# QKV of the first block in two passes of 256 tokens, its tiles normalised one by one, and the last tile's output in unequal columns on two queues: a fused attention and GLU layer on one core

## The chip, the cores and the metric

The kernel runs on one core of one Trainium2 chip. The metric is the device time of one launch in microseconds (us), the median of several launches. One run of each kernel is also profiled: the profile has every instruction of every engine with its start and its duration. A run is called slow when it is over 1.5% above the fastest run of the same kernel, else fast; the record also gives the mean clock that PE was granted in each run, as a share of full speed. PE is the tensor engine (matmuls), VectorE is DVE in the profile, ScalarE is ACT, GpSimd is POOL, and SP issues DMAs. A ratio of two kernels is the mean time of one kernel's fast runs over the mean of the other's fast runs of the same rounds on the same chip, so it is not quite the ratio of the medians that I quote.

## The reference

```python
xn = layernorm(x)                                   # x: 2048 tokens x 512
q, k, v = split_heads(xn @ wqkv)                    # 32 heads of 16
logits = q . k[pos - 2 * w] / 4, w = 0..7           # a window of 8 keys, dilation 2
s = (softmax(logits) . v[pos - 2 * w]) @ wo
h = gelu(xn @ w_gate) * (xn @ w_up)                 # 512 -> 1792
y = h @ w_down
out = x + s * silu(y)
```

All tensors are bf16. Tokens are worked on in four blocks of 512 (j = 0..3), each of four tiles of 128.

## The kernel before

Each piece of work is a task with an engine, an estimated duration and dependences. A list scheduler in the Python program runs the tasks in an imagined time and so fixes the **order** of instructions on every engine; on the chip the engines follow that order and wait for each other by semaphores. A change in one part can therefore move instructions in every later part.

The names in the profiles: tr is a transpose of a normalised tile xn_t on PE, xnT its copy. prod is a product of q and k on VectorE, and an L reduction is the 16 matmuls that add such products up to logits. sum, rs and b are the softmax's sums, their reciprocals and the spreading of these over partitions. pv is a product of attention weights and v on VectorE, and an O reduction is the 16 matmuls that add those up. In the feed-forward part (FFN), g and u are the two products with w_gate and w_up, and hT is gelu(g) * u on VectorE.

The first block's QKV, before: both halves of q, then of k, then of v; a PSUM bank holds one chunk of 128 output channels for 512 tokens, filled in two halves. The code here is shortened (`...`).

```python
def qkv(j):
    for which in range(3):                       # q, k, v
        mms = []
        if j == 0:
            for half in range(2):
                for c in range(NC):              # NC = 4 chunks
                    mms.append(add_main(2 * MM, ... qkv_mm(0, which, c, half * 256, (half + 1) * 256),
                        deps=[copied[2 * half], copied[2 * half + 1]] + [(w_there[which], 0.0)], ...))
            mms = mms[NC:]
        ...                                      # other blocks: 512 tokens at once
        for c in range(NC):
            e = add("act", ACT1, ... qkv_evacuate(j, which, c), deps=[mms[c]], ...)
```

Layer norm, before: block 0's reciprocal roots in pairs through ScalarE's square root, all other blocks' by four on GpSimd.

```python
if j == 0:
    for half in range(2):
        pair = list(ts)[2 * half : 2 * half + 2]
        r = rstd_act(pair[0], 2, [stat(t) for t in pair])
        for t in pair:
            transpose(t, norm(t, r), on_act=t % 2 == 0)
else:
    r = rstd_done[j] = rstd_pool(ts[0], TPB, [stat(t) for t in ts])
    ...
```

V goes to DRAM (vT_dram) and comes back per block and half as v_arr, four loads of 260 KB each, into three buffers, so the fourth v_arr can only be issued when the first has been used up. w_down (1.8 MB) is loaded by ScalarE's queue:

```python
start(wd_sb[:], B_w_down.rearrange("(k p) n -> p k n", p=P), q_ready[3])
```

The last tile's tail: s in two halves of 256 columns, each with its gate (silu(y) * s), its residual and its store, both stores on SP.

The softmax here doesn't subtract the row's maximum and nothing guards it: scores larger than these inputs give would overflow.

## Time and profile before

| | before |
|---|---|
| timed runs, median | 240.33 us |
| profile used for the prediction | span 242.5 us, launch 244.24 us, a slow one |
| PE busy | 94% of the span |
| VectorE busy | 65% |
| first QKV matmul / block 1's first QKV matmul | 8.39 us / 23.26 us |
| PE's waits between 70 and 97 us | about 2.8 us |

The busy shares are from the page's first line, and the last two rows are read from PE's rows of the timeline and from the list of waits. The profile was 1.6% slower than the timed runs.

### The profile page before, as it was taken

What the parts mean: (1) busy time and instruction counts of PE and PEld (TensorE: products, weight loads), DVE (VectorE), ACT (ScalarE), POOL (GpSimd) and SP (SyncE); (2) the same over time, 40 slices, a digit from 0 to 9 for tenths busy, and PEclk for the clock granted to TensorE, in tenths of its full rate; (3) what the DMA queues carried; (4) which work ended last, traced back from release to release, by engine and by line L of the source; (5) the groups of instructions that cost most, each with busy time, mean ns of one, the idle gap of its engine ahead of it and who ended that gap; (6) DMA issues with size and microseconds to landing.
All of it is one profiled execution on the core that took longest, in us unless ns stands there. A gap on an engine that the chain in (4) does not pass through costs nothing.

```text
span 242.5 us, 3469 instructions
## 1 busy us (share of the span) xinstructions
PE 228.9 (94%) x1337; PEld 106.0 (44%) x1360; DVE 157.1 (65%) x234; ACT 108.6 (45%) x162; POOL 30.2 (12%) x70
## 2 busy tenths in 40 slices
PE   7886999999988998999999999999999999999992
PEld 2675544444333433444444444444444444444441
DVE  4597999999969999996749953144342234343131
ACT  2353576477843685403683241182324142325100
POOL 7122930303332100120000000000000000000000
PEclk9999999999999999999999999999999999999999
DMA  4993799399997700091000000100000100000001
GB/s 146 347 374 133 161 205 371 86 199 311 226 288 177 167 3 0 0 195 48 23 0 3 0 0 22 43 24 0 0 1 3 43 22 22 3 0 0 22 29 39
DMA packets 14545, 22.66 MB, mean 93 GB/s; under 512 B 1328, under 2 KB 11456, under 8 KB 14528
## 3 DMA queue, kind: packets, MB, share of 16 engines
q0 software_dynamic: 2592, 8.54, 15.9%
q1 hardware_dynamic: 8208, 7.60, 10.0%
q10 hardware_dynamic: 3728, 6.29, 8.3%
q8 instruction: 10, 0.16, 0.3%
q14 instruction: 7, 0.06, 0.1%
HBM read 18.22 MB, written 4.21 MB: 92 GB/s over the span
## 4 chain that ended last, share of the span: by engine, by line
PE 78%; DVE 9%; DMA 6%; issue 2%; SPq 2%; DVEq 0%
PE y_ps L732 20%; PE u_ps L678 17%; PE g_ps L678 17%; PE qkv_ps L398 13%; DMA x_sb<-in_A_x_dram 6%; PE s_ps L720 6%; DVE prod L507 4%; PE O_ps L631 3%; PE L_ps L520 2%; DVE hT L695 2%; SPq L203 1%; DVE pv L617 1%; PE tr_ps L355 1%; SPq L198 1%; PE b_ps L584 1%
## 5 line engine op out<-in xcount | busy, mean ns | idle before, releaser
L695 DVE TENSOR_TENSOR hT<-gl,u_ps 128x512 bf16<-128x512 bf16 x56 | 38.2, 684 | 33.6 <-PE u_ps L678 28.0
L678 PE MATMUL g_ps<-xnT,wg_sb 128*128 128x512 bf16 x221 | 57.0, 379 | 1.3 <-DVE hT L695 0.8
L678 PE MATMUL u_ps<-xnT,wu_sb 128*128 128x512 bf16 x216 | 56.5, 379 | 0.4 <-issue 0.2
L688 ACT ACTIVATE gl<-g_ps 128x512 bf16<-128x512 f32 x56 | 33.4, 597 | 50.0 <-PE g_ps L678 45.3
L732 PE MATMUL y_ps<-wd_sb,hT 128*128 128x512 bf16 x218 | 50.2, 379 | 0.3
L398 PE MATMUL qkv_ps<-xnT,wqkv_sb 128*128 128x512 bf16 (+1 forms) x234 | 44.4, 336 | 3.2 <-DVE xnT L363 1.8
L617 DVE TENSOR_TENSOR pv<-attn,v_arr 128x2048 bf16<-128x2048 bf16 x32 | 37.9, 1220 | 2.8 <-DMA v_arr<-vT_dram 2.6
L507 DVE TENSOR_TENSOR prod<-q_sb,k_sb 128x2048 bf16<-128x2048 bf16 x32 | 37.8, 1217 | 0.0
L746 DVE TENSOR_TENSOR sg<-sil,s_ps 128x512 bf16<-128x512 bf16 (+1 forms) x17 | 11.0, 655 | 36.2 <-PE s_ps L720 25.0
L678 PEld LDWEIGHTS <-wg_sb 128*128 128x128 bf16 x224 | 21.5, 98 | 27.6 <-issue 2.6
L732 PEld LDWEIGHTS <-hT 128*128 128x128 bf16 x224 | 21.8, 98 | 26.7 <-issue 0.4
L678 PEld LDWEIGHTS <-wu_sb 128*128 128x128 bf16 x224 | 21.4, 98 | 26.8 <-issue 1.9
L398 PEld LDWEIGHTS <-wqkv_sb 128*128 128x128 bf16 x240 | 22.2, 98 | 20.2 <-issue 2.1
L743 ACT ACTIVATE sil<-y_ps 128x512 bf16<-128x512 f32 x16 | 9.6, 597 | 47.7 <-PE y_ps L732 47.7
L486 POOL DMA_DIRECT2D v_arr<-vT_dram x32 | 18.7, 589 | 62.2 <-DVE pv L617 37.5
L720 PE MATMUL s_ps<-wo_sb,o_sb 128*128 128x512 bf16 (+1 forms) x68 | 16.4, 367 | 0.0
L307 DVE BATCH_NORM_STATS2 stats<-x_sb 128x6 f32<-128x512 bf16 x16 | 10.8, 675 | 5.0 <-DMA x_sb<-in_A_x_dram 5.0
L411 ACT ACTIVATE q_sb<-qkv_ps 128x512 bf16<-128x512 f32 x16 | 9.2, 598 | 6.9 <-PE qkv_ps L398 6.9
L413 ACT ACTIVATE k_sb<-qkv_ps 128x512 bf16<-128x512 f32 x16 | 9.2, 599 | 4.9 <-PE qkv_ps L398 4.8
L418 ACT ACTIVATE vst<-qkv_ps 128x512 bf16<-128x512 f32 x16 | 9.1, 603 | 4.8 <-PE qkv_ps L398 4.7
L720 PEld LDWEIGHTS <-o_sb 128*128 128x128 bf16 x68 | 6.7, 98 | 7.4
L642 ACT ACTIVATE o_sb<-O_ps 128x1024 bf16<-128x1024 f32 x8 | 8.2, 1022 | 3.3 <-PE O_ps L631 2.8
(55 smaller groups left out, 116.1 us busy)
## 6 DMA issues: line engine op xcount, KB each, us to landing
v_arr<-vT_dram POOLq DMA_DIRECT2D x32, 260.0 KB, 6.9
vT_dram<-vst SPq DMA_DIRECT2D x16, 128.0 KB, 7.4
out_dram<-sg SPq DMA_DIRECT2D x15, 128.0 KB, 1.7
wg_sb<-in_B_w_gate_dram ACTq DMA_DIRECT2D x1, 1792.0 KB, 12.1
wu_sb<-in_B_w_up_dram ACTq DMA_DIRECT2D x1, 1792.0 KB, 12.7
wd_sb<-in_B_w_down_dram ACTq DMA_DIRECT2D x1, 1792.0 KB, 18.7
wqkv_sb<-in_A_wqkv_dram SPq DMA_DIRECT2D x3, 512.0 KB, 7.6
x_sb<-in_A_x_dram SPq DMA_DIRECT2D x3, 512.0 KB, 10.2
```

The source lines that it names most:

```text
L307: nc.vector.bn_stats(out=stats[:, t, :], in_=x_sb[:, t, :])
L398: nc.tensor.matmul(tiles["qkv", j, fo][:, lo:hi], lhsT=wqkv_sb[:, dk, fo * P : (fo + 1) * P], rhs=xnT[:, dk, j * TQ + lo : j * TQ + hi], s ...
L486: nc.gpsimd.dma_start(out=v_arr[32 * w4 : 32 * (w4 + 1), :, :], in_=src)
L507: nc.vector.tensor_tensor(out=prod[:], in0=tiles["q", j][:, c, :].unsqueeze(1).to_broadcast([P, 4, TQ]), in1=kwin, op=ALU.mult,)
L617: nc.vector.tensor_tensor(out=pv[:], in0=tiles["attn", j][:, w2, :].unsqueeze(1).to_broadcast([P, 4, TQ]), in1=tiles["va", j, half][:, 4 * ...
L678: nc.tensor.matmul(ps[:], lhsT=w[:, dk, fc * P : (fc + 1) * P], rhs=xnT[:, dk, j * TQ : (j + 1) * TQ], start=(dk == 0), stop=(dk == NC - 1),)
L688: nc.scalar.activation(out=tiles["gl", j, fc][:], in_=tiles["g_ps", j, fc][:], func=AF.Gelu_apprx_tanh)
L695: nc.vector.tensor_tensor(out=tiles["h", j][:, fc, :], in0=tiles["gl", j, fc][:], in1=tiles["u_ps", j, fc][:], op=ALU.mult,)
L720: nc.tensor.matmul(tiles["s", t][:, cs], lhsT=tiles["o", j][:, c, tt * P : (tt + 1) * P], rhs=wo_sb[:, c, cs], start=(c == 0), stop=(c == ...
L732: nc.tensor.matmul(tiles["y", t][:], lhsT=tiles["h", j][:, fc, tt * P : (tt + 1) * P], rhs=wd_sb[:, fc, :], start=(fc == 0), stop=(fc == N ...
L743: nc.scalar.activation(out=tiles["sil", t][:], in_=tiles["y", t][:], func=AF.Silu)
L746: nc.vector.tensor_tensor(out=tiles["sg", t][:, cs], in0=tiles["sil", t][:, cs], in1=tiles["s", t][:, cs], op=ALU.mult,)
```

## The change

The intent: keep PE fed at the start. Tiles of block 0 are normalised singly, so that the first reaches PE sooner; QKV runs all of q, k, v for the first 256 tokens, then for the second 256, with two chunks in each bank; x's second block comes in two halves, the rest of x later; three warm-up matmuls less; and, not in the change's name, block 1's roots go through ScalarE in pairs instead of GpSimd. At the end, 384 and 128 columns, the second store on ScalarE's queue, each residual right behind its gate.

```diff
-    lnpool = pool("lnpool", 3)
+    lnpool = pool("lnpool", 4)
...
     load_wqkv(0)
     load_wqkv(1)
-    load_x(1)
+    load_x(4, 6)
     load_wqkv(2)
-    load_x(2)
-    load_x(3)
+    load_x(6, 8)
+    load_x(8, 12)
+    load_x(12, 16)
...
-    for _ in range(12):
+    for _ in range(9):
         nc.tensor.matmul(warm_ps[:], lhsT=warm[:, 0:P], rhs=warm[:], start=True, stop=True)
...
         if j == 0:
+            behind = []
+            for half in range(2):
+                pair = list(ts)[2 * half : 2 * half + 2]
+                for t, s in [(t, stat(t, behind)) for t in pair]:
+                    transpose(t, norm(t, rstd_act(t, 1, [s])), on_act=t % 2 == 0)
+                behind = [copied[t] for t in pair if t % 2 == 1]
+        elif j == 1:
             for half in range(2):
                 pair = list(ts)[2 * half : 2 * half + 2]
                 r = rstd_act(pair[0], 2, [stat(t) for t in pair])
                 for t in pair:
-                    transpose(t, norm(t, r), on_act=t % 2 == 0)
+                    transpose(t, norm(t, r), on_act=False)
...
     def qkv(j):
+        w = 2 if j == 0 else 1
+        n = TQ // w
+        for lo in range(0, TQ, n):
+            for which in range(3):
+                for c in range(0, NC, w):
...                              (matmuls of w chunks into one bank, one eviction of [w, n])
...
-            nc.sync.dma_start(out=out2d[t * P : (t + 1) * P, cs], in_=tiles["sg", t][:, cs])
+            q = nc.scalar if split and cs.stop == D else nc.sync
+            q.dma_start(out=out2d[t * P : (t + 1) * P, cs], in_=tiles["sg", t][:, cs])
-        n = D // parts
-        columns = [slice(p * n, (p + 1) * n) for p in range(parts)]
+        edges = (0, D) if not split else (0, D - P, D)
+        columns = [slice(a, b) for a, b in zip(edges, edges[1:])]
```

More of the change, by code (lines that the diff above doesn't have):

```diff
@@ L177 @@
     order = Order(
-        {"xn": 3, "q": 3, "vst": 4, "va": 3, "pr": 6, "attn": 2, "o": 2, "h": 1, "gl": 3, "sg": 3,
+        {"xn": 4, "q": 3, "vst": 4, "va": 3, "pr": 6, "attn": 2, "o": 2, "h": 1, "gl": 3, "sg": 3,
          "f": 4, "a": 2, "O": 1}
@@ L200, in load_wqkv, with load_x @@
         )
-    def load_x(j):
+    def load_x(t0, t1):
         nc.sync.dma_start(
-            out=x_sb[:, j * TPB : (j + 1) * TPB, :],
-            in_=x2d[j * TQ : (j + 1) * TQ, :].rearrange("(t p) d -> p t d", p=P),
+            out=x_sb[:, t0:t1, :], in_=x2d[t0 * P : t1 * P, :].rearrange("(t p) d -> p t d", p=P)
         )
@@ L209 @@
     load_wqkv(1)
-    load_x(1)
+    load_x(4, 6)
     load_wqkv(2)
-    load_x(2)
-    load_x(3)
-    x_there = [3.2, 3.5, 3.8, 4.1] + [10.0] * 4 + [13.0] * 4 + [16.0] * 4
-    w_there = [7.0, 8.5, 11.5]
+    load_x(6, 8)
+    load_x(8, 12)
+    load_x(12, 16)
+    x_there = [3.2, 3.5, 3.8, 4.1] + [9.5] * 2 + [12.0] * 2 + [13.5] * 4 + [16.0] * 4
+    w_there = [7.0, 8.5, 11.0]
     warm = cpool.tile([P, TQ], BF16, name="warm")
@@ L291 @@
     warm_ps = psa.tile([P, TQ], F32, name="warm_ps", tag="a")
-    for _ in range(12):
+    for _ in range(9):
         nc.tensor.matmul(warm_ps[:], lhsT=warm[:, 0:P], rhs=warm[:], start=True, stop=True)
-    order.clock["pe"] = 5.6
+    order.clock["pe"] = 5.0
     copied = {}
@@ L303, in layer_norm, with stat @@
         rs = {}
-        def stat(t):
+        def stat(t, behind=()):
             def fn():
@@ L308, in fn @@
                 nc.vector.bn_aggr(out=mv[:, t, :], in_=stats[:, t, :])
-            return add("dve", STATS, fn, deps=[(x_there[t], 0.0)], prio=prio)
+            return add("dve", STATS, fn, deps=[(x_there[t], 0.0), *behind], prio=prio)
         def rstd_act(t0, n, deps):
@@ L320, in rec @@
                 nc.vector.reciprocal(out=rstd[:, t0 : t0 + n, 0], in_=rstd[:, t0 : t0 + n, 0])
-            a = add("act", 0.25, sq, deps=deps, prio=prio, func="sqrt")
-            return add("dve", 0.08, rec, deps=[a], prio=prio - 0.01)
+            a = add("act", 0.3, sq, deps=deps, prio=prio, func="sqrt")
+            return add("dve", 0.15, rec, deps=[a], prio=prio - 0.01)
         def rstd_pool(t0, n, deps):
@@ L346, in fn @@
                 )
-            return add("dve", NORM, fn, deps=[dep], prio=prio, takes=[("xn", t)])
+            return add("dve", NORM, fn, deps=[dep], prio=prio - 0.01, takes=[("xn", t)])
         def transpose(t, dep, on_act):
@@ L391 @@
     v_stored = {}
-    def qkv_mm(j, which, c, lo, hi):
-        fo = which * NC + c
-        if lo == 0:
-            tiles["qkv", j, fo] = psf.tile([P, TQ], F32, name="qkv_ps", tag="f")
-        for dk in range(NC):
-            nc.tensor.matmul(
-                tiles["qkv", j, fo][:, lo:hi],
-                lhsT=wqkv_sb[:, dk, fo * P : (fo + 1) * P],
-                rhs=xnT[:, dk, j * TQ + lo : j * TQ + hi],
-                start=(dk == 0),
-                stop=(dk == NC - 1),
-            )
@@ L406, in qkv_evacuate @@
-    def qkv_evacuate(j, which, c):
-        ps = tiles["qkv", j, which * NC + c]
-        if which == 0:
-            if c == 0:
-                tiles["q", j] = qpool.tile([P, NC, TQ], BF16, name="q_sb", tag="q")
-            nc.scalar.activation(out=tiles["q", j][:, c, :], in_=ps[:], func=AF.Copy, scale=SCALE)
-        elif which == 1:
-            nc.scalar.activation(
-                out=k_sb[:, c, PAD + j * TQ : PAD + (j + 1) * TQ], in_=ps[:], func=AF.Copy
-            )
-        else:
-            tiles["vst", j, c] = vpool.tile([P, TQ], BF16, name="vst")
-            nc.scalar.activation(out=tiles["vst", j, c][:], in_=ps[:], func=AF.Copy)
@@ L420, in qkv @@
-    def qkv(j):
-        for which in range(3):
-            mms = []
-            if j == 0:
-                for half in range(2):
-                    for c in range(NC):
-                        ts = (2 * half, 2 * half + 1)
-                        mms.append(
-                            add_main(
-                                2 * MM,
-                                lambda c=c, half=half, which=which: qkv_mm(
-                                    0, which, c, half * TQ // 2, (half + 1) * TQ // 2
-                                ),
-                                deps=[copied[t] for t in ts] + [(w_there[which], 0.0)],
-                                takes=[("f", ("qkv", 0, which, c))] if half == 0 else [],
-                            )
-                        )
-                mms = mms[NC:]
-            else:
-                for c in range(NC):
-                    mms.append(
-                        add_main(
-                            4 * MM,
-                            lambda c=c, which=which: qkv_mm(j, which, c, 0, TQ),
-                            deps=[copied[t] for t in range(j * TPB, (j + 1) * TPB)],
-                            takes=[("f", ("qkv", j, which, c))],
-                        )
-                    )
-            for c in range(NC):
-                takes = []
-                if which == 0 and c == 0:
-                    takes = [("q", j)]
-                if which == 2:
-                    takes = [("vst", (j, c))]
-                e = add(
-                    "act", ACT1, lambda c=c, which=which: qkv_evacuate(j, which, c), deps=[mms[c]],
-                    prio=-0.5, takes=takes, frees=[("f", ("qkv", j, which, c))],
-                )
-                if which == 0:
-                    q_ready[j] = e
-                elif which == 1:
-                    k_ready[j] = e
-                else:
-                    def store(c=c):
-                        nc.sync.dma_start(
-                            out=vT_dram[c * P : (c + 1) * P, PAD + j * TQ : PAD + (j + 1) * TQ],
-                            in_=tiles["vst", j, c][:],
-                        )
-                    st = add("sp", 0.6, store, deps=[e], prio=-1.0, frees=[])
-                    v_stored[j] = add(("dma", j, c), 3.0, lambda: None, deps=[(st, 0.0)], frees=[("vst", (j, c))])
@@ new lines, in store_v, with fn, mms, evacuate @@
+    def store_v(j, c, lo, n, w):
+        def fn():
+            o = vT_dram[c * P : (c + w) * P, PAD + j * TQ + lo : PAD + j * TQ + lo + n]
+            nc.sync.dma_start(
+                out=o.rearrange("(w p) n -> p w n", p=P),
+                in_=tiles["vst", j, c, lo][:].rearrange("p (w n) -> p w n", w=w),
+            )
+        return fn
+    def qkv(j):
+        w = 2 if j == 0 else 1
[3 more added lines that the diff above has]
+                for c in range(0, NC, w):
+                    key = (j, which, c, lo)
+                    def mms(key=key, which=which, c=c, lo=lo):
+                        ps = psf.tile([P, TQ], F32, name="qkv_ps", tag="f")
+                        tiles["qkv", key] = ps
+                        for i in range(w):
+                            fo = which * NC + c + i
+                            for dk in range(NC):
+                                nc.tensor.matmul(
+                                    ps[:, i * n : (i + 1) * n],
+                                    lhsT=wqkv_sb[:, dk, fo * P : (fo + 1) * P],
+                                    rhs=xnT[:, dk, j * TQ + lo : j * TQ + lo + n],
+                                    start=(dk == 0),
+                                    stop=(dk == NC - 1),
+                                )
+                    def evacuate(key=key, which=which, c=c, lo=lo):
+                        ps = tiles["qkv", key][:].rearrange("p (w n) -> p w n", w=w)
+                        if which == 0:
+                            if c == 0 and lo == 0:
+                                tiles["q", j] = qpool.tile([P, NC, TQ], BF16, name="q_sb", tag="q")
+                            nc.scalar.activation(
+                                out=tiles["q", j][:, c : c + w, lo : lo + n], in_=ps, func=AF.Copy,
+                                scale=SCALE,
+                            )
+                        elif which == 1:
+                            at = PAD + j * TQ + lo
+                            nc.scalar.activation(
+                                out=k_sb[:, c : c + w, at : at + n], in_=ps, func=AF.Copy
+                            )
+                        else:
+                            tiles["vst", j, c, lo] = vpool.tile([P, TQ], BF16, name="vst")
+                            nc.scalar.activation(
+                                out=tiles["vst", j, c, lo][:], in_=tiles["qkv", key][:], func=AF.Copy
+                            )
+                    there = [(w_there[which], 0.0)] if j == 0 else []
+                    m = add_main(
+                        4 * MM, mms,
+                        deps=[copied[t] for t in range((j * TQ + lo) // P, (j * TQ + lo + n) // P)] + there,
+                        takes=[("f", ("qkv", *key))],
+                    )
+                    takes = [("vst", key)] if which == 2 else []
+                    if which == 0 and c == 0 and lo == 0:
+                        takes = [("q", j)]
+                    e = add(
+                        "act", ACT1, evacuate, deps=[m], prio=-0.5, takes=takes,
+                        frees=[("f", ("qkv", *key))],
+                    )
+                    if which == 0:
+                        q_ready[j] = e
+                    elif which == 1:
+                        k_ready[j] = e
+                    else:
+                        st = add("sp", 0.6, store_v(j, c, lo, n, w), deps=[e], prio=-1.0)
+                        v_stored[j] = add(
+                            ("dma", key), 3.0, lambda: None, deps=[(st, 0.0)], frees=[("vst", key)]
+                        )
@@ L709, in ffn_pair, with out_tile @@
         )
-    def out_tile(j, tt, parts):
+    def out_tile(j, tt, split):
         t = j * TPB + tt
@@ L777, in add_s @@
                 add_main(
-                    4 * MM / parts, lambda cs=cs: s_mms(cs), deps=[o_ready[j]],
+                    4 * MM * (cs.stop - cs.start) / D, lambda cs=cs: s_mms(cs), deps=[o_ready[j]],
                     takes=[("f", ("s", t))] if cs.start == 0 else [],
@@ L797, in out_tile @@
             d = add(
-                "dve", 0.68 / parts, lambda cs=cs: gate(cs), deps=[a, sm], prio=-1.8,
+                "dve", 0.06 + 0.62 * (cs.stop - cs.start) / D, lambda cs=cs: gate(cs), deps=[a, sm], prio=-1.8,
                 frees=[("f", ("s", t))] if end else [],
             )
-            d = add("dve", 0.37 / parts, lambda cs=cs: residual(cs), deps=[d], prio=-1.6)
-            st = add("sp", 0.6, lambda cs=cs: store(cs), deps=[d], prio=-0.5)
+            d = add(
+                "dve", 0.06 + 0.31 * (cs.stop - cs.start) / D, lambda cs=cs: residual(cs), deps=[d],
+                prio=-1.9 if split else -1.6,
+            )
+            st = add("act" if split and end else "sp", 0.6, lambda cs=cs: store(cs), deps=[d], prio=-0.5)
             add(("dma", "out", t, cs.start), 2.0, lambda: None, deps=[(st, 0.0)], frees=[("sg", t)] if end else [])
@@ L838 @@
         for tt in range(TPB):
-            out_tile(j, tt, 2 if j == NJ - 1 and tt == TPB - 1 else 1)
+            out_tile(j, tt, j == NJ - 1 and tt == TPB - 1)
     order.run()
```

## The prediction

> **What bounds the kernel now.** I read first the page's shares, then PE's waits, then the chain of work that ended last, then the timeline of the first 30 us, and last the stretch from 66 to 97 us, where VectorE and TensorE trade places.
>
> ```profile
> PE 228.9 (94%) x1337; PEld 106.0 (44%) x1360; DVE 157.1 (65%) x234; ACT 108.6 (45%) x162; POOL 30.2 (12%) x70
> ...
> PE qkv_ps L398 <- DVE xnT L363: 1.8, 1, 1.8
> PE warm_ps L293 <- DVE eps_sb L221: 1.2, 1, 1.2
> PE qkv_ps L398 <- DMA wqkv_sb<-in_A_wqkv_dram: 1.2, 1, 1.2
> PE O_ps L631 <- DVE pv L617: 1.1, 1, 1.1
> PE tr_ps L355 <- DVE xn_t L339: 0.8, 1, 0.8
> PE g_ps L678 <- DVE hT L695: 0.8, 1, 0.8
> PE b_ps L584 <- DVE rs L578: 0.6, 1, 0.6
> ```
>
> TensorE is the bound: 94% busy, and the change takes no matmul work away (96 matmuls of 256 columns in block 0 before and after). So only idle time of PE can be won, and the list of waits says how much there is: 1.2 + 0.8 + 1.8 us before 24 us, and 0.8 + 1.1 + 0.2 + 0.6 (+0.2 issue), about 2.8 us, between 70 and 97. After 97 us PE waits for nearly nothing until the tail.
>
> ```profile
> 6.57 15.06 DMA x_sb<-in_A_x_dram
> 21.65 0.70 DVE stats L307
> 22.56 0.65 DVE xnT L363 x2
> 23.26 0.39 PE qkv_ps L398
> ...
> 237.22 0.89 PE s_ps L720 x8
> 238.11 0.04 DVEq L746
> 238.14 0.04 issue
> 238.19 0.75 DVE sg L746 x2
> 238.94 0.20 DVE sg L753
> 239.14 0.20 DVEq L866
> ```
>
> This is the chain that ended last (start, us, what). Read it backwards from 23.26: block 1's QKV waited for two copies of xnT; those stood on VectorE behind a bn_stats of x's last block, which it needed for nothing, and that waited 15 us for its DMA. The second part is the tail: PE's last s ends at 238.1, then two gates, two residuals, two stores.
>
> ```profile
> 6.48 0.71 PE L355 MATMUL tr_ps<-ident,xn_t 128*128 128x128 bf16 x8
> 7.47 0.39 DVE L363 COPY xnT<-tr_ps 128x512 bf16<-128x512 bf16 x1
> 8.39 1.05 PE L398 MATMUL qkv_ps<-xnT,wqkv_sb 128*128 128x256 bf16 x8 [1.20 <-DMA wqkv_sb<-in_A_wqkv_dram]
> 9.72 7.15 PE L398 MATMUL qkv_ps<-xnT,wqkv_sb 128*128 128x256 bf16 x64
> 17.70 0.72 PE L355 MATMUL tr_ps<-ident,xn_t 128*128 128x128 bf16 x8 [0.83 <-DVE xn_t L339]
> 23.26 1.04 PE L398 MATMUL qkv_ps<-xnT,wqkv_sb 128*128 128x512 bf16 x3 [1.77 <-DVE xnT L363]
> 69.08 1.23 DVE L617 TENSOR_TENSOR pv<-attn,v_arr 128x2048 bf16<-128x2048 bf16 x1 [2.63 <-DMA v_arr<-vT_dram]
> ```
>
> From this timeline come the unit costs: 64 matmuls of 256 columns in 7.15 us less 0.2 us of drain is 0.109 us each; four of 512 columns take 0.863 us (from the chain); four transposes some 0.2 us. On VectorE one bn_stats with its aggregation 0.80, a norm 0.36, a copy 0.36, a prod or pv 1.14, an hT product 0.60.
>
> **What the Trainium skill says.** "TensorE: Matmul & The Clock Gate", section "What's actually happening": TensorE starts at half clock and is released after a busy window of about 3.4 us, counted by free-running windows. The trace agrees: the 12 warm-up matmuls of 512 columns follow each other 0.43 us apart, later ones 0.216 us. "DMA: Bandwidth & Descriptors", section "Queues, rings and completion order": each DMA engine goes round the queues that have work, a packet at a time. That fits x's last block, 512 KB, needing 15.1 us from its issue while the 1792 KB of w_gate came in on the other queue from 9.7 us. The same page, "Issuing engines are not separate DMA queues": a second issuing engine saves only the issue time; here an issue takes 0.33 us on SP. "PSUM — Partial Sum Buffer", section "The four PSUM rules": a group's first matmul clears the accumulate bits of the whole bank; two chunks in one bank are right because one group ends before the next starts. No run here shows that.
>
> **The change, part by part.** (1) Block 0's tiles are normalised singly: 4 square roots and 4 reciprocals instead of 2 and 2, about 0.2 us more on VectorE for each pair, but tile 0 no longer waits for tile 1's statistics. Following VectorE's new order with the durations above: sqrt 0 at 4.3, norm 0 at 5.1 to 5.5, norm 1 to 6.1, copy of tile 1 at about 6.6 to 7.0 instead of 7.5 to 7.9. With three warm-ups less (3 x 0.43 = 1.3 us), PE is free from 5.1, so tile 0's transposes start at about 5.6, not 6.5. In the profile this wins nothing by itself: the first QKV matmul waits for wqkv until 8.39 anyway.
>
> (2) Two passes. PE's new order is 24 QKV matmuls, transposes of tile 2, 8, transposes of tile 3, 24, eight transposes, 16, eight, 24. From 8.39: 2.6 + 0.2 + 0.9 + 0.2 = 12.3; V's weights landed at 12.8 before with 256 KB more in front of them, so I take 12.3 for them; then 2.6 + 0.4 + 1.7 = 17.0, where tiles 6 and 7 must be normalised. VectorE reaches that at about 17.4 (statistics of 4 to 7, norms, copies, and a 1.1 us wait for the square root of tile 3, which stands on ScalarE behind the first q eviction), so 0.4 us lost; then 0.4 + 2.6 = 20.5. The copies of tiles 6 and 7 end near 19.0, so block 1 starts at 20.5, not 23.26: **2.8 us**. This rests on x in halves of 256 KB (block 1 no longer behind the whole of it) and on copies being ahead of x's last block on VectorE.
>
> (3) From there VectorE's chain. Its first score product comes at about 27 us with two copies left, which counts as 27.4 against 28.14. So VectorE is only some 0.5 to 0.7 us ahead, PE almost 3. But the new order starts the FFN with 6 pv products done and not 13, so hT is served earlier and attention put off. Walking on: 20 prods are done at 56.1, PE ends QKV near 59, hT 0 is done at 63.6, and PE finds its buffers free up to an O reduction near 72 that waits about 0.8 us. The 2.63 us for v_arr at 66.4 should vanish, since other work fills VectorE until then. So of the 2.8 us between 70 and 97, about 2 fall away.
>
> (4) The tail: the gate of 384 columns, by interpolation between 0.42 (256) and 0.69 (512), 0.55 us; the residual of 128 columns about 0.2; the last issue starts near 239.3 on ScalarE's queue instead of 239.6. **0.3 us**.
>
> Sum in the profiled run: 2.8 + 2 + 0.3, with some 0.4 from the small waits at 24 to 28 us, about 5.5 us.
>
> **What must be taken off.** The profiled run took 244.24 us and the timed ones 240.35; its span alone is 242.5. The matmuls go at their full pace in the trace, so the 3.9 us (at least 2.2) that timed runs don't spend must be idle time, and the likeliest is waiting for DMA: wqkv to 8.39, x's last block, v_arr. These are the very waits that the change is to remove. If all 3.9 are among them, only about 5.5 + 0.5 - 3.9 = 2 us are left to win; if none is, 5.5. The middle is 3.8; less the chance of the clock's rival below, I take 3.4: 240.35 - 3.4 = **236.9 us**.
>
> **Rivals.** (a) The clock. With 9 warm-ups PE is busy from 1.25 to 5.1 and then nearly idle to 8.4. If no window in this counts as busy, QKV starts at half speed and stays so for one or two windows. An estimate from the skill's 3.4 us: 3.4 to 5 us at half speed lose 1.7 to 2.5 us, leaving 1 to 2 us of gain, 238.5 to 239.5. For it: three warm-ups fewer. Against: in the kernel before the clock was up by the transposes at 6.5, and the new transposes come sooner. One chance in four. (b) VectorE takes over. If it is only 0.7 us ahead when the FFN starts, PE waits there for hT, the head's gain is given back between 60 and 97, and the time is about 239. For it: VectorE has no idle from 28 to 66 us. Against: the order moves hT forward, and v_arr's 2.63 us are slack. One in five. (c) The DMA landings stay: V's weights or tiles 6 and 7 late by 1 us or more, as w_gate is issued just when they come; 1 to 1.5 us less. (d) All of it is real in timed runs too: 234.5 to 235.
>
> **Range and chances.** 8 times in 10 between 234.6 (d) and 239.3 (a or b). Faster by over 2% means below 235.5, which needs (d) nearly whole: 0.25. Slower by over 2% would need a stall that the order doesn't show: 0.03. Within 2%: 0.72.
>
> **What would show it right or wrong.** Right: block 1's first QKV matmul near 20.5 us in the new profile; no wait of PE for xnT over 0.5 us; pv's wait for v_arr gone; PE's idle between 65 and 95 us below 1 us; last store issued 0.3 us earlier behind PE's end. Wrong on (2): block 1 after 22 us. Wrong by (a): 256-column matmuls after 8 us 0.21 us apart. Wrong by (b): PE's waits for hT or pv grown beyond 2.8 us. Wrong on the deduction: the timed runs gain as much as the profiled ones, 5 us or more.

## The result, and the profile after

The changed kernel takes **237.08 us** (236.96 to 237.75, four runs) against 240.33 us (240.01 to 240.71, four runs): ratio 0.987, 95% interval 0.9846 to 0.9893. It is 1.3% faster, clear of noise and inside the 2% band. Its profile fell in the fast state, with a span of 235.3 us.

The list of PE's waits in the changed kernel (who waited for whom: us in total, times, longest) is short:

```profile
PE qkv_ps L428 <- DVE xnT L363: 0.6, 1, 0.6
PE tr_ps L355 <- DVE xn_t L339: 0.5, 1, 0.5
PE tr_ps L355 <- DVE rstd L320: 0.4, 1, 0.4
```

Beside the 1.2 us before the first warm-up this is the whole list, and all three stand before 7.5 us. Nothing is left of the waits for hT, pv and rs between 70 and 97 us. The chain of work that ended last (start, us, what) shows the same of the head:

```profile
6.93 0.44 DVE xnT L363
7.37 0.14 issue
7.50 2.78 PE qkv_ps L428 x24
...
16.86 2.84 PE qkv_ps L428 x25
```

From 7.50 us the chain stays on PE, where before it went through x's DMA and VectorE to 23.26 us. The 25 matmuls from 16.86 are block 0's last 24 and block 1's first. Block 0's have 256 columns and block 1's 512, so a narrow view of the tile qkv_ps, from 19.25 to 19.4 us, dates block 1's first (count, ns of one as min/median/max, start of the first and of the last in us; shapes):

```profile
L428 PE MATMUL qkv_ps<-xnT,wqkv_sb x4: 273/273/379, 19.0 to 19.3; 128*128 128x256 bf16 x3, 128*128 128x512 bf16 x1
```

Block 1 starts at 19.3 us.

The difference of the two spans is 7.2 us here, and that of the timed runs 3.3 us. A comparison with the slow profile would thus have told of gains that the timed runs don't have. The first experiment settles this.

### The profile page after: what moved, and what is told of

Its sections match the earlier page's. It is cut to its first block, busy times and chain, and to the rows that moved or that the text cites. A ratio compares the mean times of both kernels' runs of the same rounds, so it can differ in the third digit from the quotient of the medians.

```text
span 235.3 us, 3474 instructions
## 1 busy us (share of the span) xinstructions
PE 226.9 (96%) x1334; PEld 105.6 (45%) x1357; DVE 158.1 (67%) x238; ACT 110.0 (47%) x166; POOL 28.2 (12%) x68
## 4 chain that ended last, share of the span: by engine, by line
PE 95%; DVE 2%; DMA 1%; issue 1%; DVEq 0%
PE g_ps L686 21%; PE y_ps L740 21%; PE u_ps L686 21%; PE qkv_ps L428 18%; PE s_ps L728 6%; PE O_ps L639 3%; PE L_ps L528 3%; PE tr_ps L355 2%; DMA x_sb<-in_A_x_dram 1%; DVE stats L307 1%; PE b_ps L592 1%; DVE xn_t L339 1%; PE sum_ps L574 0%; DVE sg L754 0%; DVE sg L761 0%
## 5 line engine op out<-in xcount | busy, mean ns | idle before, releaser
L754 DVE TENSOR_TENSOR sg<-sil,s_ps 128x512 bf16<-128x512 bf16 (+2 forms) x17 | 11.1, 654 | 34.2 <-PE s_ps L728 22.9
L740 PEld LDWEIGHTS <-hT 128*128 128x128 bf16 x224 | 21.6, 98 | 26.2 <-issue 0.4
L728 PE MATMUL s_ps<-wo_sb,o_sb 128*128 128x512 bf16 (+2 forms) x67 | 16.2, 366 | 0.0
```

Source lines behind the costliest of these rows:

```text
L728: nc.tensor.matmul(tiles["s", t][:, cs], lhsT=tiles["o", j][:, c, tt * P : (tt + 1) * P], rhs=wo_sb[:, c, cs], start=(c == 0), stop=(c == ...
L740: nc.tensor.matmul(tiles["y", t][:], lhsT=tiles["h", j][:, fc, tt * P : (tt + 1) * P], rhs=wd_sb[:, fc, :], start=(fc == 0), stop=(fc == N ...
L754: nc.vector.tensor_tensor(out=tiles["sg", t][:, cs], in0=tiles["sil", t][:, cs], in1=tiles["s", t][:, cs], op=ALU.mult,)
```

## The experiments

Twelve kernels ran; all gave the right result. "Before" beside them is the kernel before in the same rounds.

### before_again: the kernel before, unchanged

> The kernel before, unchanged, for a profile in the fast state. Time 240.3 us within 0.3 in both theories. Theory A (the profile of before was slow because DMA landed late): the span is 238 to 239 us, the first QKV matmul starts at 7.8 to 8.0 us, not 8.39, x's last block ends no idle of VectorE over 0.5 us (1.58 in the slow profile), v_arr ends less than 1.5 us (2.63), and block 1's QKV starts near 21 us, not 23.26. Theory B (the slow profile lost its time elsewhere, at the start or the end): these waits stay as in the slow profile and block 1's QKV still starts near 23 us.

Measured: 241.1 us median (240.42 to 241.63) against 240.28 for the same kernel in the same rounds, ratio 1.0028 (interval 0.999 to 1.0066): the noise of this set-up, some 0.3%, though the median is 0.8 us above what I expected. The profile is a fast one, with a span of 239.1 us. From its timeline of PE (start, us, engine, line, work), the narrow view of qkv_ps from 19.45 to 19.6 us, and its list of VectorE's and PE's waits:

```profile
7.69 1.03 PE L398 MATMUL qkv_ps<-xnT,wqkv_sb 128*128 128x256 bf16 x8 [0.81 <-ACT rstd L314]
59.99 1.03 PE L678 MATMUL g_ps<-xnT,wg_sb 128*128 128x512 bf16 x4
93.85 1.03 PE L720 MATMUL s_ps<-wo_sb,o_sb 128*128 128x512 bf16 x4
```

```profile
L398 PE MATMUL qkv_ps<-xnT,wqkv_sb x4: 272/272/379, 19.2 to 19.5; 128*128 128x256 bf16 x3, 128*128 128x512 bf16 x1
```

```profile
PE g_ps L678 <- DVE hT L695: 1.1, 1, 1.1
DVE pv L617 <- DMA v_arr<-vT_dram: 3.0, 1, 3.0
```

Theory A held for the head, by more than it said, and failed for the middle. Block 1's QKV starts at 19.5 us, not 23.26, and not near 21 as expected. (In the merged timeline this is easy to miss: one line of 11 matmuls from 18.64 us holds block 0's last 8 and block 1's first 3.) So the slow profile's head was 3.75 us longer, more than the whole 3.4 us between the spans; its DMA waits there (wqkv, x's later blocks) are gone from the fast one. But v_arr still holds VectorE for 3.0 us, and PE's waits in the middle are larger, not smaller: 1.1 + 1.1 + 0.6 + 0.2 us and 0.5 of issue, 3.5 us.

Now the two fast profiles can be set side by side, at three points on PE. The FFN of block 0 starts at 59.99 before and at 58.64 after; its end is the first s matmul, at 93.85 and at 88.41; the last tile's s starts at 233.64 and at 229.84. The stretches don't hold the same reductions, since the order changed, so I take these off (0.98 us for each L or O reduction of 16 matmuls, 0.47 for a sum with its spread):

| stretch | before_again | after | reductions in it | gain |
|---|---|---|---|---|
| to the start of the FFN | 59.99 | 58.64 | 6 / 5 | 1.35 - 0.98 = 0.4 |
| block 0's FFN | 33.86 | 29.77 | 5 and one sum / 5 | 4.09 - 0.47 = 3.6 |
| to the last s | 139.79 | 141.43 | 1 more, with a sum, after | -1.64 + 1.45 = -0.2 |
| last s to the end of the span | 5.44 | 5.41 | | 0.0 |

The sum is 3.8 us, as the spans have it. **Nearly all of it is in block 0's FFN**, a part that the change doesn't touch, and almost nothing in the head and the tail that it was made for. Of the head's 0.4 us, 0.2 are there at block 1's start (19.3 against 19.5), and they are the first QKV's earlier start (7.50 against 7.69): from there to block 1 both kernels need 11.8 us. PE went through block 0's QKV without a gap before, too, so the two passes had nothing to save there.

### before_wd_late: one load moved in the kernel before

```diff
-        start(wd_sb[:], B_w_down.rearrange("(k p) n -> p k n", p=P), q_ready[3])
+        start(wd_sb[:], B_w_down.rearrange("(k p) n -> p k n", p=P), h_ready[0, 5])
```

(The list of loads is recorded after the FFN's tasks, so that the dependence exists.) No compute instruction changes its place on any engine.

> The kernel before with w_down's load issued after the tenth gelu or so (near 73 us) instead of near 51 us, between block 3's q and k; no other instruction moves. Theory (what PE waited for between 65 and 95 us in the kernel before was a collision of transfers: w_down's 1.8 MB and the v_arr loads for block 1 are in flight together, each then takes twice as long, VectorE waits 3.0 us for v_arr and PE after it): v_arr issued near 52 us lands in 5 to 7 us instead of 10 to 12, VectorE's wait for it is below 0.5 us, PE's waits for hT, pv and rs fall from 2.8 us to under 1, and the time is 237.5 to 238.5 us. Rival (the order of VectorE's work alone makes PE wait): v_arr lands early, yet PE's waits stay above 2 us and the time within 0.5 us of 240.3.

Measured: **238.43 us** median (237.94 to 240.03) against 240.49, ratio 0.9915 (0.9881 to 0.9949); the profile's span is 236.2 us, 2.9 us below before_again. One load's place gives two thirds of what the whole change gives. The views of one tile's instructions show the loads (us from issue to landing: min, median, max). In each row the last two numbers before the semicolon are the first and the last issue in us; the line below it has the landing. In before_again, w_down and the four loads of the fourth v_arr:

```profile
L808 ACTq DMA_DIRECT2D wd_sb<-in_B_w_down_dram x1: 388/388/388, 50.6 to 50.6; - x1
...
DMA to landing us min/median/max: 16.3/16.3/16.3
```

```profile
L486 POOL DMA_DIRECT2D v_arr<-vT_dram x4: 584/584/587, 51.9 to 53.6; - x4
...
DMA to landing us min/median/max: 9.8/11.0/11.9
```

In before_wd_late, w_down and 13 v_arr loads, the fourth v_arr's among them:

```profile
L808 ACTq DMA_DIRECT2D wd_sb<-in_B_w_down_dram x1: 388/388/388, 73.8 to 73.8; - x1
...
DMA to landing us min/median/max: 8.3/8.3/8.3
```

```profile
L486 POOL DMA_DIRECT2D v_arr<-vT_dram x13: 584/584/587, 52.2 to 69.5; - x13
...
DMA to landing us min/median/max: 3.8/5.3/6.4
```

In flight together, each takes about twice as long as apart. VectorE's wait for v_arr is gone from the list, and of PE's waits after 60 us only 0.5 us for rs and 0.5 of issue are left. The stretch of block 0's FFN is 30.78 us instead of 33.86, with the same reductions in it. So the 3 us in the middle of the kernel before were a collision of two transfers, shown here by taking it away; the rival, that VectorE's order alone makes PE wait, falls.

The changed kernel avoids the same collision in another way, as its trace shows (no run put the collision back into it alone). Its order has 20 prods and 6 pv products ahead of the first hT, against 16 and 13 before, so the buffer that the fourth v_arr waits for comes free only at 60.6 us (51.9 before), when w_down, issued at 49.1, has landed. Its w_down lands after 8.6 us, and its fourth v_arr:

```profile
L494 POOL DMA_DIRECT2D v_arr<-vT_dram x4: 587/587/587, 60.6 to 62.4; - x4
...
DMA to landing us min/median/max: 3.8/4.9/5.8
```

### before_qkv_twice and after_qkv_twice: 1.73 us more for PE

Block 1's first two q chunks are computed twice in each kernel, 8 matmuls of 512 columns, order unchanged.

```diff
-        for dk in range(NC):
+        for dk in [dk for _ in range(2 if j == 1 and which == 0 and c < 2 else 1) for dk in range(NC)]:
             nc.tensor.matmul(tiles["qkv", j, fo][:, lo:hi], ...)
```

> The changed kernel with 8 matmuls of 512 columns more on PE (block 1's first two q chunks computed twice; result unchanged, order unchanged), 8 x 0.216 = 1.73 us. If PE is the bound from block 1 to the end, as I think: 237.1 + 1.7 = 238.8 us. Rival: VectorE is the bound between 60 and 97 us, PE has idle there to take the delay up, and the time rises by less than 0.9 us.

Measured: 238.54 and 238.55 in two runs, and 240.15 to 241.73 in the other four, median 240.18. The two quickest are 1.6 us above the changed kernel's quickest, 236.96, nearly the 1.73 of the matmuls, and the profile has no wait of PE after 7.5 us: PE bounds the changed kernel from QKV to its last matmul. The profiled run, 240.21, is one of the other four, and has the drop of the clock told below (mean clock 0.989). Two of the other three have the same sign, 0.988; the slowest, 241.73, has 0.998 and stays unexplained.

> The kernel before with the same 8 extra matmuls of 512 columns in block 1's q (1.73 us of PE, order unchanged). In the changed kernel they cost 1.6 us (238.54 and 238.55 against 236.96 in the runs whose clock stayed up). Theory: in the kernel before, VectorE is the bound between 65 and 97 us and PE waits 3.4 us there, so PE has room: the time rises by less than 0.6 us, and PE's waits between 65 and 97 us shrink by 1 us or more. Rival: PE bounds it too and the waits only move along: 240.3 + 1.6 = 241.9 us.

Measured: 243.49 us (242.24 to 245.87) against 240.36, ratio 1.013 (1.0086 to 1.0174). My expectation was wrong: the kernel before doesn't absorb the 1.73 us either. Its profile is 1.5 us longer than before_again, PE's waits for hT, pv, rs and prod in the middle shrank from 3.0 to 2.4 us only, and the timelines show a likely reason: both colliding loads are issued 2.2 us later, v_arr at 54.1 us instead of 51.9 and w_down at 52.8 instead of 50.6. As I read these timelines, what feeds the wait is itself fed by PE: QKV, then the products of attention, then the buffer, then v_arr, then pv and hT, then PE. A delay at the head travels through the collision. That also corrects the picture of a VectorE that bounds the middle by its own work. Two of the timed runs (244.49 and 245.87) are 2 us and more above the profiled one, with the clock up (0.996 and 1.0); I have no profile of those and leave them open.

### after_old_qkv and before_new_qkv: the two passes by themselves

The edit in outline, not word for word:

```diff
-    def qkv(j):                                  # after_old_qkv; before_new_qkv the other way round
-        for lo in range(0, TQ, n): for which in range(3): for c in range(0, NC, w): ...
+    def qkv(j):
+        for which in range(3): for half in range(2): for c in range(NC): ...
```

after_old_qkv puts the old qkv functions, shown above, into the changed kernel; before_new_qkv puts the new ones into the kernel before. Nothing else is touched by hand, but the scheduler's order follows: both have 16 prods and 13 pv products ahead of the first hT.

> The changed kernel with block 0's QKV in the old form (both halves of q, then of k, then of v; one chunk per bank); everything else as changed. If the two passes matter for the head: block 1's QKV starts 0.5 us or more later than the changed kernel's 19.5 us. Its new order puts two O reductions ahead of the FFN as the kernel before did, so by the theory that the order of VectorE's work in the middle is what pays, PE waits 1.5 us or more for hT and pv between 60 and 97 us and the time is 238.5 to 239.5 us in runs with the clock up. Rival: normalising singly and x in halves alone bring the gain: within 0.4 us of 237.1.

Measured: 241.55 us (241.03 to 242.34) against 240.36, ratio 1.0043: slower than the kernel before, 4.5 us slower than the changed kernel (in other rounds), and 2 us above the range expected. As expected the collision is back (v_arr from 53.1 us lands after 8.6 to 11.3 us, w_down after 21.6, VectorE waits 2.3 us, PE 1.3 for pv and 0.7 for rs). What I hadn't expected in this size is the head: block 1's QKV starts at 20.8 us, 1.3 later than in before_again, and the FFN at 61.60 us, 1.6 later, with three waits of PE before 11 us, of which the two longest are:

```profile
PE qkv_ps L406 <- DMA wqkv_sb<-in_A_wqkv_dram: 0.9, 1, 0.9
PE qkv_ps L406 <- DVE xnT L363: 0.8, 1, 0.8
```

The single normalisation holds tiles 2 and 3 back until tile 1 is copied; with the old QKV PE has only 16 matmuls of q to do until it needs them, with the new one 24 until tile 2 and 32 until tile 3 is to be transposed. The two parts belong together.

> The kernel before with block 0's QKV in two passes, nothing else changed. Its order still has 13 pv products ahead of the first hT (the changed kernel has 6), so by the collision theory VectorE still waits 2 us or more for v_arr and PE after it: 239.5 to 240.8 us, although PE's head is shorter or the same. Rival (two passes are what brings the gain): 238 us or less.

Measured: 240.69 us (239.9 to 243.8) against 240.49, ratio 0.9999 (0.9967 to 1.0031). (One run, 243.8, is slow and not in the ratio.) Two passes alone are worth nothing that can be measured, as the collision theory said: v_arr lands after 7.9 to 11.2 us, VectorE waits 1.5 us for it (I expected 2 or more), PE 0.8 for pv and 0.7 for rs.

### after_pairs and after_block1_pool: parts of the normalisation undone

after_pairs sends block 0 through the branch of block 1 (pairs); after_block1_pool sends block 1 through the branch with GpSimd.

```diff
-        if j == 0:                      # after_pairs: the branch for single tiles is never taken
+        if j == -1:
...
-        elif j == 1:
+        elif j <= 1:
-                    transpose(t, norm(t, r), on_act=False)
+                    transpose(t, norm(t, r), on_act=(j == 0 and t % 2 == 0))
```

```diff
-        elif j == 1:                    # after_block1_pool
+        elif j == 9:
```

> The changed kernel with block 0's tiles normalised in pairs again (through one square root each pair), all else as changed. Its order has 11 pv products ahead of the first hT, so the v_arr loads of block 1 are again issued while w_down comes in: VectorE waits 1 us or more for v_arr; the first QKV starts at 7.7 to 8.0 us instead of 7.5. 238.3 to 240 us. Rival (only the start counts): 237.3 to 237.6 us in runs with the clock up.

Measured: 238.53 us (237.57 to 238.84) against 240.49, ratio 0.9906. The time is in the expected range, but not for the reason given: the loads overlap less (w_down takes 11.6 us, v_arr issued from 55.2 us on lands after 5.1 to 8.4) and VectorE doesn't wait for v_arr. What the profile has is a first QKV at 8.01 us and the clock at half speed from 7.5 to 10.9 us. The two runs whose mean clock shows no drop took 237.57 and 238.3 us.

> The changed kernel with block 1's reciprocal roots taken for four tiles at once on GpSimd as in the kernel before, all else as changed. Block 1's QKV then waits for all four statistics and 1.3 us on GpSimd: it starts 0.5 us or more later than 19.5. 10 pv products stand ahead of the first hT, so some collision: VectorE waits 0.5 us or more for v_arr. 238 to 240 us. Rival (this part, which the change's words don't name, is worth nothing): 236.9 to 237.4 us.

Measured: 240.61 us median, but in two groups: 237.81 and 238.25, and 240.48 to 241.67. The profile belongs to 238.25. Against what I expected VectorE doesn't wait for v_arr, though the loads overlap a little (w_down takes 9.9 us, the first v_arr loads 7.0 to 8.1); block 1 starts at 20.28 us, 1.0 later than in the changed kernel, after a wait of 0.8 us for its copies. So this part, which the change's name leaves out, is worth about 1 us in the profiled state. Of the upper group, 240.48 and 240.74 have a mean clock of 0.988 and 0.989, as runs with the drop told below; 241.42 and 241.67 have 0.998, are counted as slow, and aren't explained by any profile I have.

### after_old_tail: the tail by itself

The changed kernel with two halves of 256 on SP, gate, gate, residual, residual.

```diff
-        edges = (0, D) if not split else (0, D - P, D)
+        edges = (0, D) if not split else (0, D // 2, D)
-            q = nc.scalar if split and cs.stop == D else nc.sync
+            q = nc.sync
-                prio=-1.9 if split else -1.6,
+                prio=-1.6,
```

> The changed kernel with the last tile's s in two equal halves on one queue, as before; nothing else moves. As the prediction has it (the new tail is worth 0.3 us): 237.4 us. Rival, from the profiles' tails (from the start of the last s to the end of the span 5.44 us before, 5.41 after): the tail is worth nothing, 237.1 us within 0.15, the gate again starts only after the last s matmul, and two gates stand before the two residuals.

Measured: 237.73 us median (236.66 to 239.0) against 240.28. The timed runs are spread too far for 0.3 us, but the profile decides: from the start of the last s to the end of the span it takes 5.36 us with the old tail and 5.41 with the new. **The rival held: the tail is worth nothing.** The changed kernel's last instructions:

```profile
229.84 1.04 PE L728 MATMUL s_ps<-wo_sb,o_sb 128*128 128x384 bf16 x8
230.97 0.56 DVE L754 TENSOR_TENSOR sg<-sil,s_ps 128x384 bf16<-128x384 bf16 x1 [2.75 <-PE s_ps L728]
231.56 0.36 DVE L761 TENSOR_TENSOR sg<-sg,x_sb 128x384 bf16<-128x384 bf16 x1
231.84 0.28 DVE L754 TENSOR_TENSOR sg<-sil,s_ps 128x128 bf16<-128x128 bf16 x1
232.15 0.23 DVE L761 TENSOR_TENSOR sg<-sg,x_sb 128x128 bf16<-128x128 bf16 x1
```

The first gate starts 1.13 us after the start of the last s, as before: it waits for the last of the eight s matmuls, also for those whose columns it doesn't read. Behind it the four operations now depend on each other in pairs and end 2.54 us after the start of s; before, in the order gate, gate, residual, residual, they ended after 2.29. The second queue saves the 0.3 us of issue that this costs: the last store is issued 2.57 us after the start of s in before_again and in the changed kernel.

### after_12_warm and after_fill: the clock

```diff
-    for _ in range(9):                           # after_12_warm
+    for _ in range(12):
```

> The changed kernel with 12 warm-up matmuls. If the 9 were an advantage (PE free earlier for the first transposes): QKV starts later than 7.5 us by as much as the warm-ups end after 5.65 us, about 0.7 us if the transposes of tile 0 wait for them at half clock, and the time is 237.4 to 237.8 us. If tile 1's norm at 6.45 us sets the start anyway: no change, 237.1 us. If 9 warm-ups leave the clock down in some timed runs: faster than 237.1, or less spread.

Measured: 236.89, 236.93, 236.95, 237.43, 238.27 and 239.66 us against 240.28. The best runs are those of the changed kernel, so three warm-ups more need not cost anything. But the profiled run, 239.66 us, shows one source of the spread. (It has another, too: its first QKV waited for wqkv until 8.23 us, 0.7 later than in the changed kernel.) The view by stretches (stretch: us, then busy us of PE, PEld, DVE, ACT, POOL with their instructions, PEclk, DMA share, GB/s) of after_old_tail, whose profile has the same drop, and below it a stretch of before_qkv_twice, where the clock stayed up:

```profile
4.82:8.23 3.41, 1.83 (x17) 1.15 (x16) 2.82 (x9) 0.93 (x3) 2.10 (x11) 1.00 1.01 331
8.23:11.64 3.41, 3.41 (x18) 2.37 (x17) 3.15 (x10) 1.64 (x4) 0.00 (x0) 0.50 1.09 357
```

```profile
4.49:7.91 3.41, 1.82 (x13) 0.74 (x11) 3.23 (x10) 1.19 (x3) 2.45 (x12) 1.00 1.03 340
```

PEclk is 0.50 in the second stretch: for 3.41 us PE runs at half speed, just as QKV begins, and loses half of it, 1.7 us. It happened in the profiles of after_old_tail, after_12_warm, after_qkv_twice and after_pairs, each time for exactly one window of 3.41 us, and not in the others. The window ahead of it differs. Where the clock fell, PE had been busy for 1.39 to 1.83 us of that window by this view; where it stayed up, for 1.82 us and more (1.92 in the changed kernel's own profile, 2.20 in before_again). The two sides touch at 1.82 and 1.83 us, so these 14 profiles show an edge near there and not an exact threshold of busy time. The windows start at another moment in each run (the clock first came up at 3.9 to 7.1 us in these profiles), so the same kernel can fall on one side or the other. The changed kernel sits just at the edge.

The mean clock of every run lets drops be counted. The four profiled runs with a drop have 0.989 to 0.992 and the other fast profiles 0.995 and more, so I count 0.993 and less as a drop. The changed kernel and the three kernels with the same warm-ups and block 0 (after_old_tail, after_qkv_twice, after_block1_pool) have it in 6 of 22 runs, the changed kernel's own four in none; the kernel before in 1 of 38. But the drop isn't all of the spread: 238.39 and 238.06 in after_old_tail and 238.27 in after_12_warm have clocks of 0.998 and 0.999, and stay unexplained.

after_fill puts work into that window:

```diff
             def fn():
                 tiles["tr", t] = psa.tile([P, NC * P], BF16, name="tr_ps", tag="a")
+                if t == 1:
+                    for _ in range(2):
+                        nc.tensor.matmul(tiles["tr", t][:].bitcast(F32), lhsT=warm[:, 0:P],
+                                         rhs=warm[:, 0:256], start=True, stop=True)
...
                         tiles["qkv", key] = ps
+                        if key == (0, 0, 0, 0):
+                            for _ in range(2):
+                                nc.tensor.matmul(ps[:], lhsT=warm[:, 0:P], rhs=warm[:], start=True, stop=True)
```

> The changed kernel with four more warm-up matmuls, two of 256 columns ahead of tile 1's transposes and two of 512 ahead of the first QKV matmul, all into PSUM that the next group overwrites; they stand where PE waits anyway. Theory (the drops of the clock to 0.5 for one 3.41 us window[...] cost 1.7 us in some runs): no such window in the profile, and all timed runs lie within 236.8 and 237.6 us, none near 238.6. Rival (the spread is DMA or chance): the spread stays, some runs at 238 to 239.5 us, as with 12 warm-ups.

Measured: **237.01 us, 236.83 to 237.19 in five runs**, against 240.36, ratio 0.9854 (0.9827 to 0.9881). PE is busy for 2.54 us of the window from 4.96 us, the clock stays up, and the first QKV still starts at 7.50. The median is the changed kernel's, but the spread of 2 us and more of its relatives is gone. By mean clock none of the ten runs of after_fill and after_fill_tail has a drop, where 6 in 22 would give 2.7. Ten runs are few, and the changed kernel's own four had none either, so that filling the window makes drops rarer is likely and not proven.

### after_fill_tail: a tail that does shorten the end

after_fill, with the last tile's s moved ahead of its y, and y in parts of 320 and 192 columns, each with its own PSUM bank and SBUF tiles (in outline):

```diff
-        y = add_y(); s = add_s()                         # last tile
+        sm = add_main(4 * MM, lambda: s_mms(slice(0, D)), ...)
+        for part, cs in enumerate((slice(0, 320), slice(320, D))):
+            y = add_main(NF * MM * n / D, y_part, ...)   # own bank
+            ... silu, gate, residual, store of these columns
```

> after_fill, and for the last tile s before y, and y in two parts of 320 and 192 columns, each with its own PSUM bank, silu, gate, residual and store. Theory: the tail in the changed kernel gained nothing since both gates wait for PE's last matmul and stand in series behind it; here only 192 columns are left after PE's last matmul, so the last store is issued some 1.2 to 1.4 us after PE's last y, while before it was 2.57 us after the start of the 0.86 us of s: 0.3 to 0.5 us less than after_fill, near 236.6 us. Rival: the end is set by the store's landing and the wind-down alone, or 14 narrow matmuls cost what they save: within 0.15 us of after_fill.

Measured: **236.53 us** (236.29 to 237.72, five runs) against 240.36, ratio 0.9845 (0.9816 to 0.9873). From the start of the last tile's first matmul to the end of the span it takes 7.9 us (227.3 to 235.18) instead of 8.4 (226.83 to 235.27 in after_fill): 0.5 us, as expected, since only silu, gate and residual of 192 columns stand behind PE's last matmul. The medians differ by 0.5 us too, though one of the five runs, 237.72, is above all of after_fill's. This is the fastest version: 3.8 us below the kernel before in its own rounds, where the change as given wins 3.3.

## Why the prediction was right or wrong

The time, 237.08 us, lies 0.2 from the 236.9 predicted and well within the range, and "within 2%" came. **But the sum was right with wrong terms**, so that it came so close is partly luck.

- **What bounds it (PE, only idle time to be won)** was right: with 8 matmuls more the changed kernel takes 1.6 us more, and its profile has no wait of PE after 7.5 us.
- **Step 1, single tiles**, was right in its times: square root 0 at 4.30 (predicted 4.3), norm 0 at 5.15 (5.1), transposes at 5.65 (5.6), the copy of tile 1 at 6.93 (6.6). The step's "wins nothing by itself" held only in the slow profile; with wqkv there earlier, tile 1's copy sets the start at 7.50, 0.2 us ahead of 7.69 before.
- **Step 2, the head, 2.8 us**: the walk was right, from the first QKV to block 1 12.1 us predicted and 11.8 measured. **The step that failed is what it was compared with**: 23.26 us belongs to the slow profile. The fast one starts block 1 at 19.5 and needs the same 11.8 us from its first QKV, so the gain is 0.2 us at block 1 and 0.4 by the FFN. The two passes themselves saved nothing in the head; what the step counted as their gain was DMA waits of one slow run.
- **Step 3, the middle, "about 2 fall away"**: the right thing for the right reason, hT served earlier and v_arr's wait filled by other work, but mis-sized. VectorE had no lead of 0.5 to 0.7 us from the head: its first score product came at 24.97 us with two copies left, against 24.35 with none left in the fast profile. The new order alone did it. All 3.5 us went; the corrected gain is 3.6. Predicted marks: 20 prods done at 56.1 (55.7 measured), QKV ended at 59 (58.6), hT 0 done at 63.6 (63.2), an O reduction near 72 waiting 0.8 us (it doesn't wait). And I took v_arr's landing as given; that it was late because w_down came in at the same time is what before_wd_late added.
- **Step 4, the tail, 0.3 us**: wrong. It measured 0.0; I counted the queue's gain and not that the new order chains the four operations, nor that the first gate waits for all of s. Of the prediction's signs of being right, this one failed (the last store 0.3 us earlier), and, narrowly, that no wait for xnT is over 0.5 us (0.6, at 7.5 us).
- **The deduction for the slow profile** was right in size and half right in place. The fast profile of the same kernel is 3.4 us shorter, all of it in the head, as said. But I also counted v_arr among the waits that timed runs don't have, and they do (3.0 us). So the deduction, 2.1 us from 5.5 to 3.4, took the head's excess away by a guess about all waits, and the middle's larger gain made up for it.
- **Rival (a), the clock**, given one chance in four, is real in this family of kernels (6 of 22 runs with this head) and cost about 1.6 us where it struck (240.15 to 240.22 against 238.54 in after_qkv_twice), at the low end of the estimate of 1.7 to 2.5. It didn't strike in the changed kernel's four runs. **Rival (b)**, VectorE taking over, didn't come: no wait of PE for hT or pv is left. **Rival (c)** didn't come either. **(d)** came for the middle and not for the head.

## What to carry to other kernels

When a statically ordered kernel gains in a part that the change doesn't touch, look for transfers that no longer overlap: here a new order of VectorE's work separated w_down from v_arr, and moving one load gave two thirds of it without the rest. Take a profile in the same state as the timed runs before working out what a wait is worth; a slow profile shows the right mechanisms with the wrong sizes. And when warm-up matmuls stand ahead of a gap, try filling the gap, not only the start. When a merged line of a timeline hides where a stage begins, ask for the shapes: here a stage that seemed to start at 20.8 us started at 19.5.

## What the Trainium skill lacked or had wrong

- "TensorE: Matmul & The Clock Gate", section "What's actually happening", says that the clock comes down after an idle window of about 3.4 us. The window's length agrees (3.41 us, free-running: 4.82, 8.23 and 11.64 us in one profile, and a first rise at 3.9 to 7.1 us by the run), but the window need not be idle: with PE busy for 1.39 to 1.83 us of it the clock fell to half for the next window, and with 1.82 us and more it stayed up. The page speaks further down of a kernel whose clock oscillates by short idle gaps, but it gives no busy time at which the clock falls.
- "DMA: Bandwidth & Descriptors" tells how DMA engines go round their queues (section "Queues, rings and completion order"); no page gives what it costs when two loads of one core are in flight together. Here 1.8 MB took 8.3 to 8.6 us with little beside it and 16.3 together with v_arr, and v_arr's loads of 260 KB 3.8 to 6.4 us apart and 9.8 to 11.9 together.
- No page says that a profiled run can be slow by its DMA waits alone: two profiles of one kernel had spans of 242.5 and 239.1 us, with the start of block 1's QKV at 23.26 and 19.5 us and the clock up in both.
